# Narrower mask backgrounds, query masks by multiplication, and new engine orders in a fused delta-rule attention and MLP kernel

## The chip, the cores and the metric

The kernel runs on one core of a Trainium2 chip. The metric is the device time of one execution in microseconds (us); the program is one launch from inputs in device memory to the output in device memory.

## The reference

For each of 4 batches and 8 heads a state of 48x48 is carried over 768 time steps (a delta rule with a rate beta), and the result goes through an MLP with a tanh GELU:

```python
for t in range(S):                       # q, k, v: (4, 8, 768, 48); beta: (4, 8, 768)
    y[:, :, t] = einsum('bhd,bhde->bhe', q[:, :, t], state)
    v_old = einsum('bhde,bhd->bhe', state, k_n[:, :, t])      # k_n: k by its norm
    state = state + beta_t * einsum('bhd,bhe->bhde', k_n[:, :, t], v_t - v_old)
...
x = y.transpose(0, 2, 1, 3).reshape(3072, 384)
h = x @ w_in                             # (384, 2048)
out = gelu_tanh(h) @ w_out               # (2048, 384)
```

## The kernel before

The 768 steps are cut into 12 chunks of 64 steps. A chunk c has two units, u = 2c and 2c+1; a unit holds 8 head pairs (two batches share the 128 partitions, 64 steps each). For a unit, `prep(u)` scales k by its norm (`kn`), rounds q (`qb`), turns both (on TensorE as `Th`, L585 and L599, for the first six units, by DMA as `turn` after that), and multiplies k against k and q (`G`, L619) into two PSUM banks. From the banks VectorE takes three masked triangles into SBUF: `ln` (lower, k against k), the first half of `wp` (upper, k against k) and the second half of `wp` (upper, k against q; called `wq` in the list of dependences). A triangular system is then inverted in five rounds, each a product `A` (L693), an addition from PSUM on VectorE (`rt`, `rt16`, `rt32`, L700), a product `B` (L693) and a copy of the result (`bde` or `xi`, L421, on ScalarE or VectorE). For units 0 and 1 the same five rounds run in halves (`Ath`, `rth`, `Bth`, `xih`, L661, L666). `chain(c)` carries the state: products `K`, `Um`, `Q`, `S`, `O` (L739, L775, L784, L797) and their copies; for chunk 0 it is `R0`, `Uh`, `Oh`, then a turn `Xh` (L828) with the copy `xTh` (L832). `mlp(c)` multiplies the chunk's 256 rows with W1 (`up`, L852, 16 groups of three products of 256 columns for each chunk, four groups to a GELU on ScalarE, L857) and with W2 (`down`, L864, eight groups of four products of 384 columns), and `Z` and `out` copy and store it.

The triangles are taken with `copy_predicated`, which leaves what the mask does not choose as it was. So each of the six `wp` buffers (128 partitions x 8 heads x 128) and each of the four `ln` buffers (x 64) needs a background before its first use: the unit matrix in columns 0 to 63 and zeros in the columns of `wq`. These are the operations `triw` and `tri`, copies of a template `tmpl`, 128 columns wide, whose right half is zeroed on GpSimd by `tmplz`. They may stand on ScalarE, VectorE or GpSimd. GpSimd copies two bf16 as one float. `bdz` and `bez` zero the block matrices `bd` and `be` in the same stage.

Nothing is scheduled at run time. The table `ORDER` lists for each engine every operation in its order (`pe`, `act`, `dve`, `pool`, and `sp` for the DMA queue that loads and stores); `BANKS` gives the PSUM bank of each allocation in the order of the `pe` list. Every engine works strictly through its list and waits on semaphores for what an operation needs. In a name such as `up.3.5/2`, the number is a position in the program and what stands behind the slash counts operations of one name. `fill` is a product of zeros (L476) that TensorE does between the real ones; there are 61. GpSimd's list also starts the eight loads of W1 and W2 (`w1`, `w2`, L526 and L530; `w1.-3` is the first quarter of W1, read by `up.3`). Loads into the three buffers of q, k and v are in SP's list (`loadq`, `loadk`, `loadv`; `loadqr` for the first three chunks of q), and a load waits until its buffer has been read. A second program for negative beta lies behind a flag and does not run.

Of the kernel before, what the change touches and what calls it, by code (L numbers as in the profile page):

```python
# [5 lines left out]
F32 = mybir.dt.float32  # L6
BF16 = mybir.dt.bfloat16
U16 = mybir.dt.uint16
ALU = mybir.AluOpType
# [3 lines left out]
C = 64  # L13
# [5 lines left out]
        fill/8 fill/48 fill/21 fill/20 fill/47 fill/10 fill/52 fill/13 fill/30 fill/9 fill/55 betaT.-28/0 fill/58 fill/1 fill/46  # L19
        fill/43 fill/5 fill/16 fill/27 fill/18 fill/42 fill/12 Th.0/0 fill/0 Th.1/0 fill/23 fill/4 fill/33 Gh.0/0 Gh.1/0 fill/29  # L20
        fill/45 Th.3.01/0 Ath.0/0 Ath.1/1 fill/32 fill/25 Bth.0/0 fill/7 Th.2/0 fill/39 Bth.1/1 Ath.0/2 Ath.0/1 fill/51 Ath.1/0
        Ath.1/3 G.2/0 Bth.0/1 Bth.1/0 Th.3/0 Bth.0/2 Ath.1/2 Bth.1/3 fill/36 Ath.0/3 fill/59 fill/26 Ath.0/4 Ath.1/5 G.3/0 Bth.1/2
        A.2/0 Bth.0/3 Ath.1/4 fill/31 fill/54 fill/19 Bth.1/5 Ath.0/5 Bth.0/4 Bth.1/4 Th.1.01/0 Ath.1/7 fill/60 Bth.0/5 A.3/0
        Ath.0/6 Ath.0/7 B.2/0 fill/2 Bth.1/7 fill/44 Bth.0/7 Gh.1/1 Bth.0/6 Ath.1/6 B.3/0 A.2/1 Ath.0/9 Ath.0/8 fill/37 fill/22
        fill/28 B.2/1 Th.4/0 A.3/1 Ath.1/9 Bth.0/9 Bth.1/6 Bth.0/8 fill/57 A.2/2 B.3/1 Gh.0/1 Ath.1/8 Th.5/0 bminT.40/0 Th.5.01/0
        Bth.1/8 Bth.1/9 fill/15 fill/17 A.3/2 B.2/2 Uh.0.5/0 Uh.0.5/1 G.4/0 fill/53 Oh.0.7/0 Oh.0.7/1 fill/24 B.3/2 fill/41
        Xh.0.8/0 Xh.0.8/1 A16.2/0 fill/38 G.5/0 S.0.5/0 up.3.5/0 up.3.5/1 fill/11 A16.3/0 B.2/3 A.4/0 up.3.5/2 up.3.5/3 up.3/0
        up.3/1 up.3/2 up.3/3 B.3/3 up.3.25/0 up.3.75/0 up.3.25/1 up.3.25/2 A32.2/0 up.3.25/3 B.4/0 A.5/0 A32.3/0 B.2/4 up.3.75/1
        K.2.5/0 down.4.5/0 B.3/4 up.3.75/2 down.4.54/0 up.3.75/3 A.4/1 B.5/0 fill/3 down.4/0 Um.2.5/0 A.5/1 down.4.04/0 Q.2.6/0
        O.2.7/0 S.2.5/0 down.4.58/0 down.4.62/0 fill/50 B.5/1 down.4.08/0 B.4/1 A.5/2 down.4.12/0 A.4/2 K.4.5/0 B.5/2 up.5.75/0  # L30
        B.4/2 up.5.25/0 up.5.75/1 up.5.75/2 up.5.75/3 up.5.25/1 A16.5/0 up.5.25/2 A16.4/0 up.5.25/3 G.6/0 B.5/3 up.5.5/0 up.5.5/1
        up.5.5/2 B.4/3 G.7/0 up.5.5/3 up.5/0 up.5/1 up.5/2 A32.5/0 up.5/3 A32.4/0 A.6/0 fill/34 B.5/4 A.7/0 G.9/0 G.8/0 B.4/4
        B.6/0 down.6/0 down.6.04/0 B.7/0 down.6.08/0 Um.4.5/0 A.6/1 down.6.12/0 Q.4.6/0 S.4.5/0 O.4.7/0 B.6/1 A.8/0 A.7/1
        down.6.5/0 down.6.54/0 B.8/0 A.9/0 A.6/2 down.6.58/0 B.7/1 down.6.62/0 B.9/0 A.8/1 B.6/2 A.7/2 K.6.5/0 up.7.25/0 up.7.25/1
        up.7.25/2 B.8/1 A16.6/0 B.7/2 A.9/1 up.7.25/3 up.7/0 up.7/1 B.6/3 up.7/2 A16.7/0 up.7/3 A.8/2 up.7.75/0 B.9/1 up.7.75/1
        B.7/3 up.7.75/2 A32.6/0 B.8/2 G.10/0 up.7.5/0 up.7.75/3 up.7.5/1 A32.7/0 up.7.5/2 up.7.5/3 A16.8/0 G.11/0 B.7/4 B.6/4
        B.8/3 A.9/2 down.8.5/0 down.8/0 down.8.54/0 Um.6.5/0 A.10/0 B.9/2 down.8.04/0 Q.6.6/0 S.6.5/0 O.6.7/0 A16.9/0 A.11/0
        down.8.08/0 B.10/0 A32.8/0 B.9/3 down.8.12/0 K.8.5/0 B.11/0 down.8.58/0 A32.9/0 down.8.62/0 A.10/1 B.8/4 A.11/1 B.9/4
        up.9.75/0 up.9.75/1 up.9.75/2 B.10/1 up.9.75/3 Um.8.5/0 G.13/0 up.9.25/0 up.9.25/1 up.9.25/2 up.9.25/3 Q.8.6/0 A.10/2
        B.11/1 O.8.7/0 G.12/0 S.8.5/0 up.9.5/0 up.9.5/1 up.9.5/2 up.9.5/3 up.9/0 up.9/1 up.9/2 A.11/2 up.9/3 A.13/0 K.10.5/0  # L40
        B.10/2 B.11/2 A.12/0 down.10/0 up.11/0 up.11/1 up.11/2 up.11/3 B.12/0 B.13/0 A16.10/0 up.11.25/0 down.10.04/0 B.10/3
        up.11.25/1 A16.11/0 up.11.25/2 up.11.25/3 A.12/1 A.13/1 up.11.75/0 down.10.08/0 B.11/3 up.11.75/1 A32.10/0 B.12/1 B.13/1
# [12 lines left out]
        Um.16.5/0 up.17.5/1 up.17.5/2 up.17.5/3 Q.16.6/0 G.21/0 O.16.7/0 S.16.5/0 up.17.75/0 up.17.75/1 up.17.75/2 up.17.75/3
        A.18/2 up.17/0 up.17/1 up.17/2 up.17/3 up.17.25/0 up.17.25/1 A.20/0 A.19/2 up.17.25/2 up.17.25/3 B.18/2 up.19.25/0 A.21/0
        B.20/0 B.19/2 up.19.25/1 up.19.25/2 up.19.25/3 B.21/0 up.19/0 up.19/1 A16.19/0 down.18/0 A16.18/0 A.21/1 up.19/2 up.19/3
        A.20/1 B.19/3 down.18.04/0 B.18/3 B.20/1 down.18.08/0 G.22/0 K.18.5/0 B.21/1 down.18.12/0 up.19.5/0 down.18.5/0 up.19.5/1
        A.20/2 up.19.5/2 A.21/2 up.19.5/3 A32.18/0 A32.19/0 down.18.54/0 B.20/2 B.21/2 B.19/4 down.18.58/0 B.18/4 down.20.5/0
        A16.21/0 A16.20/0 down.18.62/0 Um.18.5/0 down.20.54/0 Q.18.6/0 G.23/0 S.18.5/0 O.18.7/0 down.20.58/0 down.20/0 A.22/0  # L60
        up.19.75/0 up.19.75/1 up.19.75/2 B.20/3 up.19.75/3 A.23/0 B.22/0 down.20.04/0 B.21/3 B.23/0 K.20.5/0 A32.20/0 down.20.08/0
        A.23/1 up.21.5/0 up.21.5/1 up.21.5/2 A32.21/0 up.21.5/3 B.20/4 A.22/1 B.23/1 B.21/4 down.20.62/0 down.20.12/0 up.21.25/0
        up.21.25/1 B.22/1 A.23/2 Um.20.5/0 up.21.25/2 up.21.25/3 Q.20.6/0 B.23/2 A.22/2 S.20.5/0 O.20.7/0 up.21/0 up.21/1 up.21/2
        up.21/3 B.22/2 up.21.75/0 A16.23/0 up.21.75/1 up.21.75/2 A16.22/0 up.21.75/3 K.22.5/0 down.22/0 down.22.04/0 B.23/3 B.22/3
        down.22.08/0 up.23/0 up.23/1 up.23.25/0 up.23/2 up.23/3 down.22.12/0 A32.23/0 up.23.25/1 A32.22/0 up.23.25/2 up.23.25/3
        down.22.5/0 B.23/4 up.23.5/0 down.24.5/0 B.22/4 up.23.5/1 down.22.54/0 down.22.58/0 down.24.54/0 up.23.5/2 up.23.75/0
# [279 lines left out]
def bass_deltanet__then__act_gelu_tanh_kernel(  # L346
# [9 lines left out]
    B, H, S, D = q.shape  # L356
# [658 lines left out]
```

## Time and profile before

| | |
|---|---|
| median of 3 runs | 249.84 us (250.45, 249.84, 246.84) |
| the profiled execution | 248.81 us, of which the span from first to last instruction is 247.1 us |
| busy, TensorE (PE) | 235.5 us, 95% of the span |
| busy, VectorE (DVE) | 193.5 us, 78% |
| busy, ScalarE (ACT) | 173.0 us, 70% |
| busy, GpSimd (POOL) | 147.9 us, 60% |
| granted TensorE clock | 1.00 throughout |

A busy share is a mean over stages: in the first 40 us the kernel loads, builds the masks and inverts the first units; from then on the products of the MLP stand between those of later units. The busy time of PE includes the products of zeros.

### The profile page before, as it was taken

What the parts mean: (1) busy time and instruction counts of PE and PEld (TensorE: products, weight loads), DVE (VectorE), ACT (ScalarE), POOL (GpSimd) and SP (SyncE); (2) the same over time, 40 slices, a digit from 0 to 9 for tenths busy, and PEclk for the clock granted to TensorE, in tenths of its full rate; (3) what the DMA queues carried; (4) which work ended last, traced back from release to release, by engine and by line L of the source; (5) the groups of instructions that cost most, each with busy time, mean ns of one, the idle gap of its engine ahead of it and who ended that gap; (6) DMA issues with size and microseconds to landing.
All of it is one profiled execution on the core that took longest, in us unless ns stands there. A gap on an engine that the chain in (4) does not pass through costs nothing.

```text
span 247.1 us, 11724 instructions
## 1 busy us (share of the span) xinstructions
PE 235.5 (95%) x5222; PEld 184.3 (75%) x5239; DVE 193.5 (78%) x340; ACT 173.0 (70%) x285; POOL 147.9 (60%) x224
## 2 busy tenths in 40 slices
PE   7778887999999999999999999999999999999995
PEld 3356776868878977888777888777887788877772
DVE  5999997888999999887898897999788897710200
ACT  6788887847988986877766795855684547655260
POOL 4099976659587888687879695985947332020000
PEclk9999999999999999999999999999999999999999
DMA  5999999999999998999979599728584012400142
GB/s 106 179 175 168 159 167 175 173 140 119 162 168 133 156 177 146 167 122 167 144 123 145 114 141 150 105 48 113 96 178 69 20 35 47 104 3 3 27 104 72
DMA packets 105063, 29.62 MB, mean 120 GB/s; under 512 B 96784, under 2 KB 104976, under 8 KB 105008
## 3 DMA queue, kind: packets, MB, share of 16 engines
q1 hardware_dynamic: 100640, 25.37, 65.9%
q0 software_dynamic: 3712, 3.15, 9.4%
q8 instruction: 43, 0.70, 1.3%
q10 hardware_dynamic: 656, 0.30, 0.5%
q14 instruction: 12, 0.10, 0.2%
HBM read 20.55 MB, written 4.72 MB: 102 GB/s over the span
## 4 chain that ended last, share of the span: by engine, by line
PE 87%; DVE 6%; ACT 2%; issue 2%; POOL 1%; POOLq 0%
PE ps L852 26%; PE ps L864 26%; PE ps L693 20%; PE ps L739 3%; PE ps L619 3%; PE ps L476 2%; PE ps L775 2%; PE ps L797 2%; PE ps L661 2%; PE ps L784 1%; DVE rt L700 1%; DVE nrm L546 1%; DVE rl L666 1%; POOL xi L650 1%; DVE wp L627 1%
## 5 line engine op out<-in xcount | busy, mean ns | idle before, releaser
L852 PE MATMUL ps<-xT,W 128*128 128x256 bf16 x576 | 77.5, 272 | 0.0
L864 PE MATMUL ps<-W,gT 128*128 128x384 bf16 x384 | 74.7, 326 | 0.4 <-issue 0.4
L421 ACT ACTIVATE bd<-ps 64x512 bf16<-64x512 f32 (+2 forms) x115 | 62.9, 561 | 12.6 <-PE ps L693 10.7
L857 ACT ACTIVATE gT<-ps 128x1024 bf16<-128x1024 f32 x48 | 48.7, 1021 | 19.7 <-PE ps L852 19.3
L852 PEld LDWEIGHTS ps<-xT,W 128*128 128x128 bf16 x576 | 50.7, 97 | 6.8
L700 DVE TENSOR_TENSOR rt<-ps,two 128x512 bf16<-128x512 f32 x66 | 44.1, 684 | 6.1 <-PE ps L693 5.4
L864 PEld LDWEIGHTS ps<-W,gT 128*128 128x128 bf16 x384 | 33.1, 97 | 16.8 <-issue 0.6
L687 POOL COPY be<-xi 64x256 f32<-64x256 f32 (+1 forms) x64 | 24.1, 382 | 31.5 <-ACT xi L421 19.0
L421 DVE CAST bd<-ps 64x512 bf16<-64x512 f32 (+2 forms) x41 | 26.3, 649 | 5.2 <-PE ps L693 4.7
L700 DVE TENSOR_TENSOR rl<-ps,two 128x384 bf16<-128x384 f32 (+1 forms) x44 | 20.8, 486 | 9.4 <-PE ps L693 8.8
L549 POOL TENSOR_TENSOR nrm<-nrm,half 128x16 f32<-128x16 f32 x9 | 26.4, 2936 | 2.8 <-DVE nrm L546 2.6
L683 POOL TENSOR_SCALAR_AFFINE_SELECT be<-ln 64x512 bf16<-64x512 bf16 x32 | 21.9, 684 | 10.2 <-DVE ln L640 5.5
L643 DVE CAST_PREDICATED wp<-mup,ps 128x1024 bf16<-128x1024 uint16 x22 | 26.7, 1212 | 0.5 <-PE ps L619 0.3
L421 ACT ACTIVATE xi<-ps 128x256 bf16<-128x256 f32 (+2 forms) x40 | 19.1, 492 | 10.8 <-PE ps L693 8.6
L576 POOL TENSOR_TENSOR tok<-kraw,nrm 128x384 bf16<-128x384 f32 x22 | 18.2, 832 | 6.6 <-PE ps L784 5.2
L693 PE MATMUL ps<-wp,be 128*128 128x64 bf16 (+1 forms) x384 | 18.2, 187 | 0.4 <-issue 0.3
L640 DVE CAST_PREDICATED ln<-mlo,ps 128x512 bf16<-128x512 uint16 x22 | 15.0, 687 | 4.5 <-PE ps L619 4.3
L693 PEld LDWEIGHTS ps<-wp,be 128*128 128x128 bf16 x384 | 15.5, 97 | 2.5 <-issue 0.6
L476 PE MATMUL ps<-wz 128*128 128x512 bf16 x44 | 14.4, 433 | 2.4 <-DVE braw L482 1.3
L421 ACT ACTIVATE ob<-ps 128x384 f32<-128x384 f32 x16 | 7.8, 489 | 12.4 <-PE ps L864 12.2
L693 PE MATMUL ps<-ln,bd 128*128 128x64 bf16 (+1 forms) x352 | 15.9, 188 | 0.1
L693 PEld LDWEIGHTS ps<-ln,bd 128*128 128x128 bf16 x352 | 13.8, 97 | 1.6
(119 smaller groups left out, 368.2 us busy)
## 6 DMA issues: line engine op xcount, KB each, us to landing
vraw<-in_v_dram SPq DMA_DIRECT2D x24, 192.0 KB, 4.8
out_dram<-ob SPq DMA_DIRECT2D x47, 96.0 KB, 3.1
kraw<-in_k_dram SPq DMA_DIRECT2D x22, 192.0 KB, 4.9
qraw<-in_q_dram SPq DMA_DIRECT2D x18, 192.0 KB, 5.1
W<-in_moe_w_out_dram POOLq DMA_DIRECT2D x4, 384.0 KB, 6.9
W<-in_moe_w_in_dram POOLq DMA_DIRECT2D x4, 384.0 KB, 6.5
qraw<-in_q_dram SPq DMA_DIRECT2D x12, 96.0 KB, 3.6
kraw<-in_k_dram SPq DMA_DIRECT2D x3, 96.0 KB, 3.6
```

What stands on the lines that cost most here:

```text
L421: return e.activation(out, in_, ACT.Copy) if e is nc.scalar else e.tensor_copy(out, in_)
L476: return e.matmul(P(f"fill{i}")[:, :], wz[:, 0:128], wz[:, 0:512])
L549: e.tensor_tensor(nr[:, 1, hx], nr[:, 0, hx], half[:, hx], ALU.pow),
L576: A("dve" if u < 2 else POOL, z + "kn", lambda e, P: e.tensor_tensor(kn, kr, nr[:, 3, hx].rearrange("t (p g) -> t p g", p=2).unsqueeze(3). ...
L643: A("dve", z + "wp", lambda e, P: e.copy_predicated(wp[s][:, :, :], mup[:, :].bitcast(U16).unsqueeze(1).to_broadcast([128, H, 2 * C]), P(p ...
L683: A("pool", z + "X1", lambda e, P, src=src, dst=dst: e.affine_select(out=dst, in_=src, compare_op=ALU.not_equal, fill=-1.0, base=0, patter ...
L687: A("pool", z + "bdc", lambda e, P, src=src, dst=dst: e.tensor_copy(dst.bitcast(F32), src.bitcast(F32)), reads=[w("xi")], writes=[xs[a]], ...
L693: ins = e.matmul(P(name)[:, C * h + to.start:C * h + to.stop], D_[:, h, :], rhs[:, h, to])
L700: A("dve", z + f"rt{lo or str()}", lambda e, P, i=i, to=LIVE[i], r_=r_: e.tensor_tensor(r_[:, :, to], P(ps(f"A{i}")).rearrange("p (h t) -> ...
L852: ins = e.matmul(P(ph)[:, w * f:w * f + w].rearrange("p (x t) -> p x t", x=2), W1[:, j, 128 * (i + f):128 * (i + f) + 128], x_[:, :, j, :] ...
L857: A("act", z + "gelu", lambda e, P, i=i, ph=ph: e.activation(g_[:, i:i + nf, 0:w], P(ph).rearrange("p (f t) -> p f t", f=nf), ACT.Gelu_app ...
L864: ins = e.matmul(P(po)[:, 0:DM], g_[:, f, 128 * b:128 * b + 128], W2[:, f, :], start=(f == 0), stop=(f == FC - 1))
```

## The change

The template is 64 columns wide and has no zero half, so `tmplz` is gone and `triw` writes columns 0 to 63 of a `wp` buffer only, 512 elements in a partition in place of 1024. In the first use of each buffer (units 0 to 5) the second half of `wp` is no longer taken with `copy_predicated`: it is multiplied with the mask, which writes zeros where the mask is zero and needs no background. For units 0 and 1 this replaces one operation by one (`wph`). For units 2 to 5 the one operation `wp` over 1024 elements becomes two over 512, `wp` and `wq`. From unit 6 on nothing is different: a buffer has its zeros from the first use.

```diff
-        tmpl = sb("tmpl", [128, 2 * C])
+        tmpl = sb("tmpl", [128, C])
...
-                A("pool", "0tmplz", lambda e, P: e.memset(tmpl[:, C:2 * C], 0.0), writes=["tmplz"], pos=-11)
...
-            for t, n, w in ((ln, "ln", C), (wp, "wp", 2 * C)):
+            for t, n, w in ((ln, "ln", C), (wp, "wp", C)):
...
-                        e, t[s][:, :, :], tmpl[:, 0:w].unsqueeze(1).to_broadcast([128, H, w])) if e is not nc.gpsimd else
-                      e.tensor_copy(t[s][:, :, :].bitcast(F32), tmpl[:, 0:w].bitcast(F32).unsqueeze(1).to_broadcast([128, H, w // 2])),
-                      reads=["tmpl", "tmplz"], writes=[f"{n}{s}"] + ([f"wq{s}"] if w > C else []), pos=2 * s - 9)
+                        e, t[s][:, :, 0:w], tmpl[:, 0:w].unsqueeze(1).to_broadcast([128, H, w])) if e is not nc.gpsimd else
+                      e.tensor_copy(t[s][:, :, 0:w].bitcast(F32), tmpl[:, 0:w].bitcast(F32).unsqueeze(1).to_broadcast([128, H, w // 2])),
+                      reads=["tmpl"], writes=[f"{n}{s}"], pos=2 * s - 9)
...
-                A("dve", z + "wph", masked(wp[s][:, :, C:2 * C], mup[:, 0:C], ps("Gq")), reads=["mup"], frees=[ps("Gq")], writes=[n("wq")], pos=u)
+                A("dve", z + "wph", lambda e, P: e.tensor_tensor(wp[s][:, :, C:2 * C].rearrange("p (x g) t -> p x g t", x=2), head(P(ps("Gq"))),
+                                                                 mup[:, 0:C].unsqueeze(1).unsqueeze(1).to_broadcast([128, 2, 4, C]), ALU.mult),
+                  reads=["mup"], frees=[ps("Gq")], writes=[n("wq")], pos=u)
...
+                if u < NP:
+                    gcols = lambda P, y: P(ps("G")).rearrange("p (h t) -> p h t", h=H)[:, :, C * y:C * y + C]
+                    A("dve", z + "wp", lambda e, P: e.copy_predicated(
+                        wp[s][:, :, 0:C], mup[:, 0:C].bitcast(U16).unsqueeze(1).to_broadcast([128, H, C]), gcols(P, 0)), reads=["mup"], frees=[ps("G")], writes=[n("wp")], pos=u)
+                    A("dve", z + "wq", lambda e, P: e.tensor_tensor(
+                        wp[s][:, :, C:2 * C], gcols(P, 1), mup[:, 0:C].unsqueeze(1).to_broadcast([128, H, C]), ALU.mult), reads=["mup"], frees=[ps("G")], writes=[n("wq")], pos=u)
+                else:
...
```

All five lists of `ORDER` and the table `BANKS` are replaced. Of the lists two lines stand for the rest:

```diff
-        masks.-12/1 masks.-12/0 half.-28/0 masks.-12/2 tmplz.-11/0 ident.-29/0 mup.-12/0 mup.-12/1 two.-12/0 ident2.-29/0
...
+        masks.-12/0 masks.-12/1 masks.-12/2 two.-12/0 two.-12/1 ident.-29/0 ident2.-29/0 mlo.-12/0 triw.-9/0 mlo.-12/1 triw.-7/0
...
```

There are 61 products of zeros in both. Between ScalarE, VectorE and GpSimd 116 operations change sides, most of them copies out of PSUM. Of the ten backgrounds `tri` and `triw`, GpSimd had one before and has seven now (five `triw`, two `tri`); ScalarE has the other three, and VectorE, which had four, has none.

Three places show what moves. The first is VectorE's list from the first use of the mask of unit 2 (`ln2`, `wp2`) to that of unit 3; `rt`, `xi` and `nrm` are other work, and the numbers behind names are those of buffers. Before:

```order
L640 COPY_PREDICATED ln2<-mlo0,ps 128x512
L643 COPY_PREDICATED wp2<-mup0,ps 128x1024
L421 CAST xi0<-ps 128x256
L666 TENSOR_TENSOR rt1<-ps,two0 128x256
L666 TENSOR_TENSOR rt0<-ps,two0 128x256 x2
L640 COPY_PREDICATED ln3<-mlo0,ps 128x512
L551 TENSOR_SCALAR nrm2<-nrm2 128x16
L700 TENSOR_TENSOR rt2<-ps,two0 128x512
L666 TENSOR_TENSOR rt1<-ps,two0 128x256 x2
L553 RECIPROCAL nrm2<-nrm2 128x16
L666 TENSOR_TENSOR rt0<-ps,two0 128x256
L643 COPY_PREDICATED wp3<-mup0,ps 128x1024
```

and now:

```order
L642 COPY_PREDICATED ln2<-mlo0,ps 128x512
L649 TENSOR_TENSOR wp2<-ps,mup0 128x8x64
L647 COPY_PREDICATED wp2<-mup0,ps 128x8x64
L675 TENSOR_TENSOR rt1<-ps,two0 128x256 x2
L675 TENSOR_TENSOR rt0<-ps,two0 128x256
L642 COPY_PREDICATED ln3<-mlo0,ps 128x512
L675 TENSOR_TENSOR rt0<-ps,two0 128x256
L647 COPY_PREDICATED wp3<-mup0,ps 128x8x64
...
L709 TENSOR_TENSOR rt2<-ps,two0 128x512
L649 TENSOR_TENSOR wp3<-ps,mup0 128x8x64
```

One operation of twice the width became two; for unit 3 the query half now comes later than the other.

The second is the head of GpSimd's list, up to the first `X1h` (L650 before, L659 now; it makes `xi` of unit 0). Before:

```order
L439 AFFINE_SELECT mup<-mup 64x128 x2
L446 AFFINE_SELECT two<-two 64x64
L429 AFFINE_SELECT ident<-ident 128x128
L446 AFFINE_SELECT two<-two 64x64
L443 AFFINE_SELECT mlo<-mlo 64x64 x2
L650 TENSOR_TENSOR xi<-ln,two 128x256
L555 TENSOR_TENSOR nrm<-nrm,bsb 128x16
```

and now:

```order
L462 COPY wp<-tmpl 128x8x32
L444 AFFINE_SELECT mlo<-mlo 64x64
L462 COPY wp<-tmpl 128x8x32
L436 MEMSET half 128x16
L470 MEMSET bd 128x1024
L440 AFFINE_SELECT mup<-mup 64x128
L530 DMA W<-in_moe_w_out_dram 128x4x384
L462 COPY ln<-tmpl 128x256
L555 TENSOR_TENSOR nrm<-nrm,bneg 128x8
L440 AFFINE_SELECT mup<-mup 64x128
L462 COPY wp<-tmpl 128x8x32 x2
L659 TENSOR_TENSOR xi<-ln,two 128x256 x3
```

Backgrounds (L462), the zeroing of a `bd` (L470), a step of unit 1's norms (L555) and the first load of W2 (L530) now stand ahead of it.

The third is TensorE's list around the first products with W1 (L852 before, L861 now), which wait for the copies `xTh` of the turned chunk 0 (L828, L837). Before:

```order
L828 MATMUL ps<-ident,xo 128x128 x6
L693 MATMUL ps<-ln,bd 128x48 x8
L476 MATMUL ps<-wz 128x512
L619 MATMUL ps<-kT 64x128 x16
L784 MATMUL ps<-us,tok 64x48 x32
L852 MATMUL ps<-xT,W 128x256 x6
```

and now:

```order
L837 MATMUL ps<-ident,xo 128x128 x6
L476 MATMUL ps<-wz 128x512
L861 MATMUL ps<-xT,W 128x256 x6
L619 MATMUL ps<-kT 64x128 x16
L702 MATMUL ps<-rl_2,bd 128x64 x8
L702 MATMUL ps<-ln,bd 128x48 x8
L861 MATMUL ps<-xT,W 128x256 x18
```

The first products of the MLP now stand ahead of `G` of unit 5 (L619) and of the state's product `S` (L784, further down now).

267 lines of the change are left out of this document (134 added, 133 removed), and 16 rows, old and new, of the table BANKS.

## The prediction

> **What bounds the kernel now.** I read the page's busy shares first, then its slices, then the busy time by stage, because the change touches the first 40 us only in its arithmetic but every stage in its orders.
>
> ```profile
> span 247.1 us, 11724 instructions
> PE 235.5 (95%) x5222; PEld 184.3 (75%) x5239; DVE 193.5 (78%) x340; ACT 173.0 (70%) x285; POOL 147.9 (60%) x224
> ...
> PE   7778887999999999999999999999999999999995
> ...
> DVE  5999997888999999887898897999788897710200
> ```
>
> TensorE is full from the seventh slice on, VectorE is full in slices 2 to 6. The stages, cut where this turns (first columns: length, then busy time and count of PE, PE weight loads, DVE, ACT, POOL):
>
> ```profile
> 10.00:34.00 24.00, 20.47 (x558) 15.36 (x568) 23.86 (x62) 20.31 (x48) 20.80 (x25) 1.00 1.15 167
> 34.00:40.00 6.00, 4.35 (x142) 3.24 (x141) 4.38 (x9) 4.89 (x10) 3.37 (x6) 1.00 1.29 184
> 40.00:50.00 10.00, 9.95 (x210) 8.56 (x209) 9.15 (x16) 8.35 (x12) 6.92 (x8) 1.00 1.41 167
> 50.00:75.00 25.00, 24.32 (x616) 19.02 (x616) 22.83 (x33) 19.11 (x30) 18.19 (x26) 1.00 1.01 146
> 75.00:100.00 25.00, 24.80 (x611) 20.55 (x609) 23.65 (x39) 21.04 (x36) 21.18 (x27) 1.00 1.03 157
> 100.00:125.00 25.00, 24.68 (x551) 20.61 (x549) 20.85 (x33) 19.75 (x30) 18.70 (x31) 1.00 1.02 149
> 125.00:243.00 118.00, 117.88 (x2527) 93.43 (x2526) 81.82 (x129) 72.66 (x110) 56.12 (x89) 1.00 0.47 83
> ```
>
> From 10 to 34 us VectorE works 23.86 of 24.00 us: this stage is as long as VectorE's list up to there. From 40 to 243 us TensorE idles 0.05 + 0.68 + 0.20 + 0.32 + 0.12 = 1.37 of 203 us: this stage is as long as TensorE's real work, which the change leaves alone. So only three things can move the end: when TensorE becomes full, the 1.37 us, and products of zeros that stand between real ones. In the 40 us before, PE's busy time is no work measure, since 44 recorded products of zeros are in it:
>
> ```profile
> L476 PE MATMUL ps<-wz 128*128 128x512 bf16 x44 | 14.4, 433 | 2.4 <-DVE braw L482 1.3 <-issue 0.5 <-DVE bsb L492 0.4
> ```
>
> **The change part by part.** First VectorE's stretch. It runs from the copy of the first turned k (`kTh` of unit 0) to the copy of the turned chunk 0 (`xTh`), behind which the MLP's first products stand in both orders:
>
> ```profile
> 10.96 0.42 DVE L421 COPY kT<-ps 128x512 bf16<-128x512 bf16 x1
> 37.82 0.56 DVE L421 COPY xT<-ps 128x384 bf16<-128x384 bf16 x2
> ```
>
> that is 26.86 us. What is in it, by rows:
>
> ```profile
> L643 DVE CAST_PREDICATED wp<-mup,ps 128x1024 bf16<-128x1024 uint16 x22 | 26.7, 1212 | 0.5 <-PE ps L619 0.3
> L627 DVE CAST_PREDICATED wp<-mup,ps 128x512 bf16<-128x512 uint16 x2 | 1.4, 686 | 0.0
> L700 DVE TENSOR_TENSOR rt<-ps,two 128x512 bf16<-128x512 f32 x66 | 44.1, 684 | 6.1 <-PE ps L693 5.4
> L752 DVE TENSOR_TENSOR rs<-ps,vraw 128x768 bf16<-128x768 f32 x11 | 10.5, 951 | 0.4 <-PE ps L739 0.4
> L421 DVE COPY wp<-tmpl 128x1024 bf16<-128x1024 bf16 x3 | 1.2, 422 | 0.6 <-ACT tmpl L456 0.6
> L421 DVE CAST bd<-ps 64x512 bf16<-64x512 f32 x21 | 14.4, 684 | 1.7 <-PE ps L693 1.4
> L421 DVE CAST xi<-ps 128x256 bf16<-128x256 f32 x4 | 1.7, 414 | 0.0
> L421 DVE COPY kT<-ps 128x512 bf16<-128x512 bf16 x3 | 1.2, 414 | 0.0
> L472 DVE MEMSET be<- 128x512 uint32 x2 | 1.0, 485 | 0.1
> ```
>
> The multiplication `wq` is not in this trace. Its bounds are a copy without PSUM, 0.42 us for twice the width, and the 768-wide operation from PSUM, 0.95 us; I take 0.684 us, the addition `rt`, which has the same width, the same source in PSUM and a second operand repeated over the heads. The narrower `wp` is 0.686 us. So a first use of units 2 to 5 costs 0.684 + 0.686 - 1.212 = +0.16 us, 0.63 us for all four (by the bounds -0.42 to +1.70), and for units 0 and 1 nothing (0.684 for 0.686). Three of the four lie in the stretch: +0.48. The new list puts three more `bde` there (+2.05) and one `binv` (0.17), and takes out one `xih` (0.41), one `kTh` (0.41), one wide background (0.42), one `bez` (0.48) and one reciprocal (0.24). The sum is +0.74 us of durations. All durations of the stretch add up to 31.0 us in 26.86 us of time, as neighbours overlap, so 0.74 counts 0.64; I take **+0.6**, with -0.5 and +1.5 as ends from the bounds of `wq`.
>
> Before the stretch VectorE was not full: what set the time was ScalarE, whose backgrounds stood ahead of the first squares. From the chain of waits:
>
> ```profile
> 4.05 0.63 ACT ln L421
> 4.68 0.95 ACT wp L421
> 5.63 0.42 ACT sq L544
> 6.07 0.55 DVE nrm L546
> ```
>
> The two backgrounds leave ScalarE's place here and go to GpSimd, whose list had nothing to do until 12.65 us. That frees 1.58 us, but the squares need k:
>
> ```profile
> 0.79 0.74 ACTq L518 DMA_DIRECT2D kraw<-in_k_dram  x1
> 1.57 0.63 ACTq L483 DMA_DIRECT2D braw<-in_beta_dram  x1
> ...
> kraw<-in_k_dram ACTq DMA_DIRECT2D x1, 96.0 KB, 3.1
> ```
>
> ScalarE now issues beta ahead of its piece of k, so this starts near 1.57 and lands near 4.7, and SP has a piece of q ahead of the others. The first square can start about 0.7 us earlier than at 5.53, the second (its pieces are SP's third and fourth, one issue later) not. VectorE does three more zeroings (`bdz`, 0.48 each) here, in time in which it waited. I take **-0.5** for `kTh`; the ends are -1.4, where only VectorE's own list counts, and +0.8, one issue on SP, where the second k pieces decide.
>
> Then the turn into the full stage:
>
> ```profile
> 38.33 0.41 PE L619 MATMUL ps<-kT 48*64 48x128 bf16 x13
> 39.85 0.25 PE L619 MATMUL ps<-kT 48*64 48x128 bf16 x3 [1.11 <-issue]
> ```
>
> TensorE stops 1.11 us inside `G` of unit 5, between two products that wait for nothing; no engine releases it. What it is, the trace does not say; I suppose that instructions came late. It can come again at another place or not at all, so I count half: **-0.55** (0 to -1.1). In the new order the first products with W1 stand ahead of this `G`, which only exchanges work within a full engine. Behind the first `up` there were five products of zeros before the last ones of the program, now there are four; three of them cost 0.65 us in the chain:
>
> ```profile
> 11.04 0.65 PE ps L476 x3
> ```
>
> so **-0.2**. Work that moves between engines after 40 us I cost at nothing: it is covered by TensorE's full queue, and without the cover each us of idling there is a us of time.
>
> Sum: +0.6 - 0.5 - 0.55 - 0.2 = -0.65 us. The profiled execution took 248.81 us with 247.1 us of span; the sum on it gives 248.2. It lies 1.0 below the median shown, 249.84, and the mean of it and the three runs is 249.0, which I take as base: **248.3 us**.
>
> **The rivals.** *(a) The early W2 load holds up k.* GpSimd now starts a quarter of W2 behind the sixth piece of its list; from the release of the template at 4.05 us and what stands between I estimate 6.5 us, where it was 20.7 at the earliest. How loads fare without and with weights in flight show the issues from 5 to 15 us and from 18 to 36 us (size, us to landing):
>
> ```profile
> kraw<-in_k_dram SPq DMA_DIRECT2D x6, 192.0 KB, 4.2
> ...
> W<-in_moe_w_in_dram POOLq DMA_DIRECT2D x4, 384.0 KB, 6.5
> kraw<-in_k_dram SPq DMA_DIRECT2D x3, 192.0 KB, 8.0
> ...
> ACT sq L544 <- DMA kraw<-in_k_dram: 0.9, 1, 0.9
> ```
>
> The square of chunk 1 waited 0.9 us for k already, and now stands ahead of `kTh` of unit 1 on ScalarE and of all of VectorE's masks. If k of chunk 1, issued about 4 to 5.3 us, takes 8.0 instead of 4.2 us, it lands at 13.3, 3.3 us behind 10, from where on it decides: 248.3 + 3.3 = 251.6. For it speaks the doubled landing, against it that this k has a lead of more than 1 us. In the Trainium skill, "DMA: Bandwidth & Descriptors", section "Queues, rings and completion order", each DMA engine takes turns between the queues that have work, a packet at a time; by that rule any load beside the weights loses about half its rate, whoever was first. The landing times agree (8.0 for 4.2); by it alone the rival would be the forecast, were the weights issued together with k.
>
> *(b) The cover breaks in the full stage.* From 40 to 125 us VectorE works 76.5 of 85 us. New orders and new banks can put TensorE behind copies that come late; a twentieth of these 85 us is +4.3: 252.6 or more. Against it: the totals by engine hardly move (VectorE gains 0.63 and loses three backgrounds of 0.42).
>
> *(c) Everything comes.* Head -1.4, gap -1.1, zeros -0.2, stretch 0, idling of the full stage -1.2: 249.0 - 3.9 = 245.1. Against it: VectorE's stretch got longer by count.
>
> *(d) Nothing comes.* The second half of k decides, and the gap stays: 0.6 - 0.2 = +0.4: 249.4.
>
> **How the numbers follow.** The forecast has 0.45 (its own range 246.8 to 249.9), (a) 0.17, (b) 0.10, (c) 0.13, (d) 0.15. The low end, 245.0, is (c); the high end, 253.4, holds (a) and half of (b). A measurement of this kernel can tell about 2% from no change, 5 us. Faster by that needs all of (c) and a little more: 0.07. Slower needs the worse half of (b), or (a) with a second delay: 0.13. Within: 0.80.
>
> **What would show it.** Right: first `up` between 37.5 and 39.5 us (40.34 before), `kTh` of unit 0 near 10.4, `wq` 0.68 and narrow `wp` 0.69 us, VectorE over 95% busy from 11 to 34 us, TensorE idle under 1.6 us from 40 to 243. Wrong: a wait of ScalarE or VectorE on a k load before 16 us (a), PE idle of several us after 40 (b), or VectorE with gaps before 34 us, which would mean that another engine, GpSimd with its longer list, sets the first stage.

## The result, and the profile after

The change makes the kernel slower by a little over one per cent: 253.0 us median of 20 runs (249.67 to 258.62) against 248.21 us (246.84 to 250.45, 20 runs); the ratio is 1.0115, with a 95% interval from 1.0084 to 1.0146. The forecast was 248.3 us, slightly faster than the 249.0 that it took as base. Ten of the change's 20 runs, the profiled one of 254.62 us among them, stand more than 1.5% above its fastest and are left out of the ratio, which is therefore smaller than that of the medians (1.019).

The page's head and slices for the changed kernel:

```profile
span 252.9 us, 11719 instructions
PE 236.5 (94%) x5225; PEld 184.9 (73%) x5239; DVE 194.7 (77%) x341; ACT 170.0 (67%) x283; POOL 148.7 (59%) x228
...
PE   7788866989999997999999999999999999999995
...
PEclk9999988999999999999999999999999999999999
```

The work is the same (PE 236.5 us busy for 235.5), the span is 5.8 us longer, TensorE has holes in slices 6, 7 and 16, and its granted clock is below full in slices 6 and 7, which it is nowhere in the profile before. By stage (length, then busy time and count of PE, PE weight loads, DVE, ACT, POOL; granted clock, DMA share, GB/s):

```profile
10.00:34.00 24.00, 20.96 (x551) 14.82 (x558) 23.52 (x58) 18.99 (x47) 19.15 (x27) 1.00 1.08 177
34.00:40.00 6.00, 3.76 (x98) 3.05 (x99) 3.55 (x8) 3.47 (x6) 2.22 (x2) 0.72 1.45 171
40.00:50.00 10.00, 7.85 (x164) 6.24 (x165) 6.56 (x13) 6.97 (x11) 5.29 (x9) 1.00 1.29 173
50.00:75.00 25.00, 24.09 (x545) 19.00 (x544) 21.84 (x35) 18.48 (x30) 18.95 (x21) 1.00 0.78 125
75.00:100.00 25.00, 23.36 (x646) 19.55 (x644) 21.83 (x34) 20.96 (x35) 20.86 (x30) 1.00 0.96 147
100.00:125.00 25.00, 24.80 (x577) 20.35 (x573) 20.79 (x33) 19.46 (x32) 19.90 (x31) 1.00 0.81 140
125.00:243.00 118.00, 117.88 (x2591) 95.06 (x2591) 88.30 (x140) 73.39 (x113) 56.57 (x93) 1.00 0.49 85
```

Up to 34 us all is as forecast: VectorE is full (23.52 of 24.00). Then every engine has holes at once, between 34 and 50 us, so no engine is waiting for a busier one. From 40 to 243 us TensorE idles 2.15 + 0.91 + 1.64 + 0.20 + 0.12 = 5.02 us, where it was 1.37. Where it stops, by the timeline of TensorE (start, length, what, count, and in brackets the idle time ahead):

```profile
36.29 0.22 PE L670 MATMUL ps<-rl,xi 64*64 64x64 bf16 x2 [1.58 <-issue]
...
41.92 0.81 PE L861 MATMUL ps<-xT,W 128*128 128x256 bf16 x6 [0.28 <-ACT xT L422]
...
44.70 0.36 PE L619 MATMUL ps<-kT 48*64 48x128 bf16 x12 [1.79 <-issue]
...
51.55 0.71 PE L861 MATMUL ps<-xT,W 128*128 128x256 bf16 x5 [0.86 <-issue]
...
99.14 0.38 PE L806 MATMUL ps<-us,wp 64*64 64x48 bf16 x25 [1.50 <-issue]
```

The second of these lines is the first `up`; the other four are stops. Each of them is in the midst of a group of equal matmuls, and no engine releases it: it is the stop of 1.11 us at 39.85 us in the profile before, four times, 5.73 us in sum. The account nearly closes: the first `up` starts at 41.92 instead of 40.34 us (+1.58; that this is also the size of the first stop is chance, since the clock told of below enters too), and from 40 us on TensorE idles 3.65 us more, of which some 0.3 us lie ahead of that `up`: together about 5 of the 5.8 us.

What the stops have in common shows when the time is cut where TensorE resumes. The counts of PE and PE weight loads between two resumptions, for the changed kernel:

```profile
36.28:44.69 8.41, 5.60 (x125) 4.26 (x126) 4.37 (x9) 4.63 (x9) 3.22 (x5) 0.80 1.39 170
44.69:51.54 6.85, 5.99 (x126) 5.12 (x127) 5.91 (x11) 6.00 (x8) 3.61 (x6) 1.00 1.31 171
51.54:99.13 47.59, 45.89 (x1136) 37.25 (x1138) 42.59 (x65) 37.52 (x61) 37.40 (x47) 1.00 0.86 137
```

That is 251, 253 and 2274 = 9 x 252.7 instructions. TensorE stops after about 253 recorded instructions or a multiple of it (a few records and the waits are missing in the count). The profile also has a DMA queue for instructions, here for the whole program and for the 1.6 us from 33.2 us on, in which the first of the stops begins:

```profile
q8 instruction: 42, 0.69, 1.2%
```

```profile
q1 hardware_dynamic: 756, 0.14, 84.1%
q0 software_dynamic: 99, 0.10, 58.6%
q8 instruction: 1, 0.02, 5.8%
```

42 packets of 16 KB carry TensorE's 5225 + 5239 instructions, 66 bytes each: one packet is one block of about 250 instructions, and the packets come all through the run. (The Trainium skill, "Trainium Architecture — The Big Picture", section "The software stack", has instructions of 64 bytes; the 66 here agree, as a few records are missing in the count.) In the second window one packet is served beside loads that keep the DMA engines at 84% + 59%; 5.8% of 16 engines and 1.6 us is 1.48 us for this packet. By the trace's list of packets it starts at 33.26 us, TensorE reaches the end of its block at 34.7 and resumes at 36.29; for the other three stops the packet starts at 41.39, 48.67 and 96.49 us. TensorE resumes 2.7 to 3.3 us behind the start, as in the profile before (packet 36.87, resumed 39.85); over the stops of 0.4 us or more in all profiles it is 2.2 to 3.6 us.

On top comes the clock. TensorE in the 8 us around the first stop, changed kernel:

```profile
34.00:36.00 2.00, 0.71 (x15) 1.00 1.38 163
36.00:38.00 2.00, 1.35 (x31) 0.62 1.35 200
38.00:40.00 2.00, 1.69 (x56) 0.53 1.63 150
40.00:42.00 2.00, 1.64 (x33) 1.00 1.42 192
```

The means 0.62 and 0.53 make 1.52 + 1.88 = 3.4 us at half clock, at once behind the stop, from 36.48 to 39.89 us; up to 1.7 us of work at full clock are lost there. The Trainium skill, "TensorE: Matmul & The Clock Gate", section "What's actually happening", tells of a window of 3413 ns that runs freely, after an idle one of which TensorE gets half clock. The length agrees. That a whole window must be idle does not: the stop here is 1.58 us, and TensorE was at work on both sides of it. Nor is it the length of the stop alone, since the longer one of 1.79 us is not followed by half clock. Cut into stretches of 3.41 us, counted from 36.48 us, where the half clock begins, the profile shows why (length, then busy time of PE first):

```profile
33.07:36.48 3.41, 1.83 (x53) 1.04 (x51) 1.84 (x4) 2.22 (x4) 3.15 (x2) 1.00 1.39 175
43.31:46.72 3.41, 2.02 (x40) 1.80 (x41) 1.60 (x3) 1.26 (x3) 0.59 (x2) 1.00 1.18 150
```

The stretch ahead of the half clock holds 1.58 us of idle time; the stop of 1.79 us is cut by the border at 43.31, and the stretch behind that border holds 1.39 us. Cut in the same way, the profiles below show half clock behind every stretch with 1.6 us or more of idle time and full clock behind every one with 1.5 us or less; with 1.58 us they show both. (The run with SP's list alone, told of below, is left out: there half clock once followed 1.14 us.)

### The profile page after: what moved, and what is told of

It reads as the page before. It is cut to its first block, busy times and chain, and to the rows that moved or that the text cites. A ratio compares the mean times of both kernels' runs of the same rounds, so it can differ in the third digit from the quotient of the medians.

```text
span 252.9 us, 11719 instructions
## 1 busy us (share of the span) xinstructions
PE 236.5 (94%) x5225; PEld 184.9 (73%) x5239; DVE 194.7 (77%) x341; ACT 170.0 (67%) x283; POOL 148.7 (59%) x228
## 4 chain that ended last, share of the span: by engine, by line
PE 82%; DVE 11%; issue 4%; POOL 1%; ACT 0%; POOLq 0%
PE ps L873 25%; PE ps L861 24%; PE ps L702 19%; PE ps L748 3%; PE ps L619 3%; PE ps L784 2%; PE ps L806 1%; PE ps L476 1%; DVE rt L709 1%; DVE rt L675 1%; PE ps L793 1%; PE ps L670 1%; DVE bd L470 1%; POOL be L692 1%; DVE wp L649 1%
## 5 line engine op out<-in xcount | busy, mean ns | idle before, releaser
L861 PE MATMUL ps<-xT,W 128*128 128x256 bf16 x576 | 77.3, 272 | 1.1 <-issue 0.9
L873 PE MATMUL ps<-W,gT 128*128 128x384 bf16 x384 | 73.8, 326 | 0.0
L422 ACT ACTIVATE bd<-ps 64x512 bf16<-64x512 f32 (+2 forms) x111 | 60.6, 564 | 18.0 <-PE ps L702 16.6
L861 PEld LDWEIGHTS ps<-xT,W 128*128 128x128 bf16 x576 | 50.7, 98 | 8.4 <-issue 1.0
L696 POOL COPY be<-xi 64x224 f32<-64x224 f32 (+1 forms) x64 | 24.6, 391 | 28.6 <-ACT xi L422 22.3
L692 POOL TENSOR_SCALAR_AFFINE_SELECT be<-ln 64x512 bf16<-64x512 bf16 x32 | 21.0, 657 | 18.4 <-DVE ln L642 11.5
L422 DVE CAST bd<-ps 64x512 bf16<-64x512 f32 (+2 forms) x45 | 28.3, 639 | 3.5 <-PE ps L702 3.0
L652 DVE CAST_PREDICATED wp<-mup,ps 128x1024 bf16<-128x1024 uint16 x18 | 21.8, 1210 | 0.7 <-PE ps L619 0.7
L476 PE MATMUL ps<-wz 128*128 128x512 bf16 x47 | 15.9, 424 | 2.3 <-DVE wz L428 1.9
L702 PE MATMUL ps<-wp,be 128*128 128x64 bf16 (+1 forms) x384 | 17.1, 188 | 0.3 <-POOL be L696 0.2
L702 PE MATMUL ps<-ln,bd 128*128 128x48 bf16 (+1 forms) x352 | 15.9, 188 | 0.0
L758 POOL TENSOR_TENSOR vraw<-vraw,bsb 128x768 f32<-128x768 f32 x9 | 13.3, 1474 | 2.7 <-DMA vraw<-in_v_dram 2.4
```

Of the source, the lines that this page charges most:

```text
L422: return e.activation(out, in_, ACT.Copy) if e is nc.scalar else e.tensor_copy(out, in_)
L476: return e.matmul(P(f"fill{i}")[:, :], wz[:, 0:128], wz[:, 0:512])
L652: A("dve", z + "wp", lambda e, P: e.copy_predicated(wp[s][:, :, :], mup[:, :].bitcast(U16).unsqueeze(1).to_broadcast([128, H, 2 * C]), P(p ...
L692: A("pool", z + "X1", lambda e, P, src=src, dst=dst: e.affine_select(out=dst, in_=src, compare_op=ALU.not_equal, fill=-1.0, base=0, patter ...
L696: A("pool", z + "bdc", lambda e, P, src=src, dst=dst: e.tensor_copy(dst.bitcast(F32), src.bitcast(F32)), reads=[w("xi")], writes=[xs[a]], ...
L702: ins = e.matmul(P(name)[:, C * h + to.start:C * h + to.stop], D_[:, h, :], rhs[:, h, to])
```

## The experiments

Four theories. **A, late instructions:** the new order runs through its blocks of 250 instructions faster than the next ones come while loads keep the DMA engines full. **B, VectorE's stretch:** the four operations more on VectorE delay the first stage. **C, the early W2 load** (rival (a) of the prediction). **D, the stops belong to the work at which they stand.** Ratios below are to the kernel before, measured on the same chip.

**Arithmetic and orders apart.** First the new sums in the old orders and banks:

```diff
  lists and banks of the kernel before, code of the changed one; pool: -tmplz.-11/0
  dve:  wp.2/0 +wq.2/0   wp.3/0 +wq.3/0   wp.4/0 +wq.4/0   wp.5/0 +wq.5/0
```

> The orders and banks of before with the narrow backgrounds and the multiplied query masks alone (each wq stands right behind its wp, and the zeroing of the template's right half is left out). Theory, late instructions: the changed kernel lost its time in stops of TensorE at every 256th of its instructions, which come from the orders; this kernel should stop as before does, and take the time of before to within 1 us, 247.5 to 249.3. Rival, VectorE's stretch: the four wq at 0.68 us make the first stage longer than the prediction counted; then this kernel takes 250.5 or more, most of the loss of the change.

249.56 us, ratio 1.0016 (0.9976 to 1.0056): 0.3 us above what A expected, and 0.9 below what B did. Then the old sums in the new orders:

```diff
  lists and banks of the changed kernel, code of the one before; pool: +tmplz.-11/0
  dve:  -wq.2/0 -wq.3/0 -wq.4/0 -wq.5/0
```

> The orders and banks of the change with the old masks (wide backgrounds, no wq, the template zeroed on GpSimd). Theory, late instructions: stops of 1 to 2 us of TensorE at instructions 1209, 1463 and 1719 as in the changed kernel, and a time of 251 to 254. Rival, VectorE's stretch: 248 to 249, the time of before, since the multiplications are gone.

253.48 us, ratio 1.0148 (1.0079 to 1.0217). The arithmetic costs nothing that can be measured and the loss is that of the orders: B falls. The stops over 0.5 us in the second kernel's waits (engine, line, releaser; total, times, longest) and the stage in which its clock fell:

```profile
PE ps L811 <- issue: 1.7, 1, 1.7
PE ps L675 <- issue: 0.6, 1, 0.6
```

```profile
75.00:100.00 25.00, 23.26 (x543) 0.93 0.84 135
```

Two of the change's four stops are there: L675 is the group of its first, L811 that of its fourth. At the other two places TensorE runs on, though A expected them all. In the first kernel, which has TensorE's list of before, there are stops too, 1.54, 0.56 and 0.55 us, at the ends of other blocks than the one at 39.85 us, and none is followed by a lower clock. So the end of a block is a place where a stop can come, and it does not come there in every run.

**The early W2 load.**

```diff
  pool:  mup.-12/0 -w2.-1.7/0 tri.-9/0 ... w2.-1.9/0 +w2.-1.7/0 eps.6/0
```

> The changed kernel with the early load of a quarter of W2 moved from the seventh place behind the masks to the end of the eight weight loads. Rival, early weights: k of chunk 1 lands sooner, the copy of the first turned k starts nearer 9.5 us, and the time falls by 2 to 3 us. Theory, late instructions: the stops behind 34 us stay and the time is that of the changed kernel to within 1 us (its undisturbed runs were about 251.4).

252.54 us, ratio 1.0083 (1.0037 to 1.0129): the interval overlaps that of the change (1.0084 to 1.0146). Of C little or nothing is left; stops of 1.79 us at 41.81 us and 2.16 us at 97.28 us remain, at the places of the change's second and fourth.

**SP's list alone.**

```diff
  lists and banks of the changed kernel, but sp: the list before;
  act: -loadk.-40/0 +loadk.-40/1
```

> The changed kernel with the loads and stores of the DMA queue in the order of before. If instructions are late because the changed order of loads puts more traffic in their way between 28 and 52 us, the stops at instructions 1209, 1463 and 1719 shrink to what before has (one of 1.1 us) and the time falls by 2 to 4 us, to about 249. If they are late because TensorE's own list reaches the end of its blocks sooner, the stops stay and the time stays within 1 us of the changed kernel.

281.51 us, ratio 1.1288 (1.1218 to 1.1358), which nobody had expected and which says little on the question. The waits of TensorE and GpSimd:

```profile
PE ps L716 <- POOL be L710: 14.9, 3, 6.1
```

```profile
POOL tok L436 <- DMA qraw<-in_q_dram: 12.0, 3, 5.2
...
POOL sq L559 <- DMA kraw<-in_k_dram: 7.0, 1, 7.0
```

Loads stand in SP's list behind stores that the other lists now finish later; GpSimd waits for q and k, and TensorE for GpSimd. The lists only fit together as a set, so the order of the loads alone is not told apart. TensorE's list alone was not tried either, so whether it is TensorE's order or that of the loads that makes the stops stays open.

**Quiet DMA engines.** The loads of chunks 3 and later are cut to a sixteenth, in the changed kernel and in the one before; every instruction of every engine stays.

```diff
-                    js = slice(0, 2 * H) if x is None else slice(x, 2 * H, 2)
+                    js = (slice(0, 2 * H) if c < 3 else slice(0, 1)) if x is None else slice(x, 2 * H, 2)
```

> The changed kernel, whose loads of q, k and v for chunks 3 and later bring one head column of sixteen (so most of the input is left out of the computation; every instruction of the engines stays). Theory 'late instructions': TensorE's instructions come in blocks of 256 (128 matmuls) over the same DMA engines as the data, a block that TensorE runs through in about 4 us while loads are heavy ends before the next block is there, and in the changed kernel the blocks between 30 and 55 us are the shorter ones. With little loaded the blocks come at once: the stops without releaser of over 0.5 us (5.7 us in the profile of the change) fall to under 1.5 us in sum, no stretch at half clock, 247 to 249. Rival 'the order itself' (TensorE's list is so arranged that it waits, loads or not): the stops stay, 251 to 254.

> The kernel before with the same loads cut (chunks 3 and later bring one head column of sixteen; the rest of the input is left out). Theory 'late instructions': its stops of 1.1 and 0.35 us go, 246 to 247.5, so that the changed kernel with the same cut stands within 1.5 us of it, where without the cut 3 lay between them. Rival 'the order itself': 248, and the distance of some 3 us to the changed kernel stays.

247.55 us, ratio 0.9956 (0.9928 to 0.9984), and 248.08 us, ratio 0.9933 (0.9894 to 0.9971): the intervals overlap, so the two kernels no longer differ by more than the noise, though the second lies 0.6 us above what A expected of it. In the profile of the one before no stop without a releaser over 0.3 us is left; but three of its 12 runs have a mean clock of 0.993, so a stop that brings half clock still came in some. The stages of the changed one, and the largest stops in its waits:

```profile
34.00:40.00 6.00, 5.63 (x155) 4.09 (x150) 5.08 (x12) 5.24 (x12) 4.32 (x6) 1.00 1.12 159
40.00:50.00 10.00, 10.00 (x218) 8.32 (x216) 9.29 (x16) 9.56 (x14) 8.32 (x10) 1.00 0.51 77
```

```profile
PE ps L819 <- issue: 1.3, 1, 1.3
```

The three stops between 34 and 52 us are gone, TensorE is full from 40 to 75 us, and none of the 12 runs of the changed kernel had a stretch at half clock. This is the plainest answer: with all loads the new orders cost 1.15%, with few loads nothing that can be measured. The fourth stop stays (1.28 us, resumed at 92.11), however, and stays at the same matmuls of the same `O` group. The DMA engines from 86 to 91 us, in 40 slices:

```profile
DMA  3210299770000000000000000006000000000000
...
q1 hardware_dynamic: 160, 0.11, 11.6%
q8 instruction: 1, 0.02, 1.5%
```

They are idle from 87.3 us on; the single 6 is the packet of instructions, at 89.5 us, 3.4 us after TensorE had entered the block before (86.1). So full DMA engines are not the only thing that makes a block start late.

**Other ends of the blocks.** 32 small matmuls ahead of the first warm-up matmul (`fill/60` in the changed kernel, `fill/8` in the one before) move all ends by 64 instructions:

```diff
             def fill(e, P, i):
+                for x in range(32 if i == 60 else 0):
+                    e.matmul(P(f"fill{i}")[:, 0:8], wz[:, 0:128], wz[:, 0:8])
                 return e.matmul(P(f"fill{i}")[:, :], wz[:, 0:128], wz[:, 0:512])
```

> The changed kernel with 32 matmuls of 8 columns ahead of its first warm-up matmul, in time in which TensorE waits anyway; all blocks of 256 instructions then begin 64 instructions earlier in the work. From the starts in the profile of the change (stops taken out) the block that then begins at about 51 us takes 2.3 us to run, where 4.0 is the shortest there without the shift, and one near 110 us takes 1.9. Theory 'late instructions': the stops at 36, 45 and 52 us leave their places in the work and stand 64 instructions earlier, new ones of 1.5 to 3 us come at the ends of those two short blocks, 255 to 258. Rival 'the stops belong to the work at which they stand' (a wait that the profile does not show): they stay at the same matmuls, 252.5 to 253.5.

> The kernel before with the same 32 small matmuls ahead of its first warm-up matmul. Its blocks between 30 and 50 us keep 4 to 6 us each, but the one that then begins at about 51 us takes 3.3 us, and one near 108 us 1.5. Theory 'late instructions': the stop of 1.1 us at 39.85 us leaves its place, new ones of 1 to 3 us come at the ends of the two short blocks, 250 to 253. Rival 'the stops belong to the work': 248 to 249.

258.38 us, ratio 1.0409 (1.0356 to 1.0461), and 255.63 us, ratio 1.0250 (1.0194 to 1.0305). These 0.9 us of small matmuls cost 2.9% in the changed kernel (1.0409 by 1.0115) and 2.5% in the one before, twice what the whole change does. A part may be the head: `kTh` of unit 0 comes at 11.24 for 10.14 us in the changed kernel, and at 11.21 for 10.96 us in the one before. The largest stops of the kernel before, shifted:

```profile
33.75 0.55 PE L601 MATMUL ps<-ident,tok 128*128 128x128 bf16 x7 [0.64 <-issue]
...
38.70 0.26 PE L695 MATMUL ps<-rt,bd 128*128 128x64 bf16 x3 [0.81 <-issue]
...
56.67 0.21 PE L786 MATMUL ps<-us,tok 64*64 64x48 bf16 x3 [1.63 <-issue]
...
108.41 0.22 PE L786 MATMUL ps<-us,tok 64*64 64x48 bf16 x4 [0.73 <-issue]
...
179.97 0.21 PE L786 MATMUL ps<-us,tok 64*64 64x48 bf16 x3 [1.58 <-issue]
```

The old stop at `G` of unit 5 is gone, new ones came, the largest at the end of the block that begins at 51 us, as expected (3.3 us to run). The last one shows something that A does not have: the packet started at 177.53 us, 1.7 us after TensorE had entered the block before, no later than most, and from 177.8 us on the DMA engines are nearly idle; but that block took only 2.5 us to run. So a short block can end in a stop though its successor is not held up by loads. Another of 0.88 us stands at 132.31, and in the changed kernel three of 0.45 to 0.69 us stand behind 130 us. In the changed kernel the largest is 2.74 us, at 40.86 us, and the two blocks named as short end in stops of 1.05 us (58.35) and 0.69 us (111.40), smaller than the 1.5 to 3 expected. Its counts between resumptions are 254, 759 = 3 x 253 and 2023 = 8 x 252.9, though the stops stand at other matmuls: D falls. The shifted kernels cost more than the stops in their one profile add up to (the changed one: 5.4 us more by median, 3.0 by the spans of the profiles). The clock, at 0.987 or below in four of its six runs, has a part in it.

**Filling the stop.** Four warm-up matmuls ahead of the first stop, between 32.2 and 33.6 us, are done three times:

```diff
             def fill(e, P, i):
+                if i in (36, 11, 17, 3):
+                    for x in range(2):
+                        e.matmul(P(f"fill{i}")[:, :], wz[:, 0:128], wz[:, 0:512])
```

> The changed kernel; four of its warm-up matmuls between 32.2 and 33.6 us (0.22 us each) are done three times, so that TensorE has 1.76 us more to do in the block of instructions at whose end the profile of the change shows the stop of 1.58 us and, after it, 3.41 us at half clock. Theory 'late instructions, and half clock on top where the stop is long': the next block comes when it did, so the added matmuls only fill the stop; it shrinks to under 0.6 us, the matmuls after it start between 36.0 and 36.6 us as before, and the half clock at 36.5 to 39.9 us falls away, which is worth up to 1.7 us: 251 to 253, and more of the runs at a mean clock of 1.0 (3 of 20 for the change). Rival 'the stop belongs to the work': stop and added matmuls add up, 254.5 to 255.5.

253.89 us, ratio 1.0215 (1.0168 to 1.0262). Between the two expectations, and no gain:

```profile
36.78 0.19 PE L705 MATMUL ps<-wp,bd 128*128 128x64 bf16 x1 [1.33 <-issue]
...
97.43 0.18 PE L796 MATMUL ps<-us,tok 64*64 64x48 bf16 x1 [1.61 <-issue]
```

```profile
36.50:40.00 3.50, 2.92 (x108) 1.00 1.39 186
96.00:98.00 2.00, 0.57 (x40) 1.00 1.09 163
98.00:100.00 2.00, 2.00 (x36) 0.51 0.21 46
100.00:102.00 2.00, 2.00 (x60) 0.64 0.68 116
```

The 1.76 us of added matmuls went mostly into the stop: TensorE resumes 0.5 us later than in the change, and the clock stays full there. But the stop is still 1.33 us, not under 0.6, since the next packet came no earlier; and the half clock (0.98 + 0.72 = 1.7 us lost) came behind the stop at 97.43 us instead. All six runs had such a stretch. Filling this one stop with products of zeros did not buy back what it costs.

**A shift the other way.** The first eight warm-up matmuls become 120 small ones, so that the ends move by 224, which is 32 instructions the other way:

```diff
+                if i in (60, 10, 2, 25, 13, 9, 55, 26):
+                    for x in range(14):
+                        e.matmul(P(f"fill{i}")[:, 0:8], wz[:, 0:128], wz[:, 0:8])
+                    return e.matmul(P(f"fill{i}")[:, 0:8], wz[:, 0:128], wz[:, 0:8])
```

> The changed kernel; its first eight warm-up matmuls of 512 columns are replaced by 120 of 8 columns (together 3.4 us as before), so that the ends of all blocks move by 224 instructions, which is 32 the other way. From the starts in the profiles no block between 30 and 60 us then takes less than 4.0 us (3.9 in the change, 2.3 with the shift by 64). Theory 'what counts is which work falls into one block': 251 to 254, as the change itself. Rival 'more instructions, or more small matmuls at the start, cost by themselves' (64 of them went with 5.4 us): 224 cost more than that, 258 or above.

257.25 us, ratio 1.0367 (1.0309 to 1.0425): my expectation of 251 to 254 fails, and the rival's 258 is missed by less than 1 us, so that more instructions at the start cost something by themselves is not excluded. (The profiled execution, 254.75 us, was the shortest of the six; where the others lost 1 to 5 us more no trace shows.) The largest stops:

```profile
37.06 0.21 PE L778 MATMUL ps<-rs,xi 64*64 64x48 bf16 x2 [2.06 <-issue]
...
77.06 0.34 PE L810 MATMUL ps<-us,wp 64*64 64x48 bf16 x18 [1.42 <-issue]
99.19 0.25 PE L810 MATMUL ps<-us,wp 64*64 64x48 bf16 x9 [1.84 <-issue]
```

The first stands at the end of a block that took about 4.7 us to run, longer than many that pass without a stop; its packet started at 34.60 us, 4.3 us after TensorE had entered the block. So the length of a block does not decide alone. Over all profiles the start comes 0.2 to 5.1 us after the entry (mostly 1 to 2; 2.5 to 5.1 ahead of the stops between 30 and 50 us), and a stop is about this delay plus 3 us less the block's own length. What sets the delay is not settled: quiet DMA engines shorten it (at most 2.9 us up to 80 us in the kernel with small loads), but not everywhere.

**The clock by runs.** Each run's span was recorded with its mean clock, and a stretch of 3.4 us at half clock lowers the mean by 0.007. 45 runs of the kernel before were taken beside the first eight experiments, not beside those of the change (a forty-sixth took 785 us and is left out): 39 had no such stretch (0.996 or above), with a mean span of 247.0 us, and six had one (0.990 to 0.993), with 250.2 us. So half clock comes in the kernel before too, in one run of eight. Of the change's 20 runs four had none (249.6 us), eight one (0.991 to 0.993; 250.3 us), seven two (0.985 to 0.987; 253.7 us) and one three (256.9 us): 251.7 us in the mean, 4.7 above the 247.0. Some 2.6 us of it stand in runs without half clock (only four, from 247.9 to 253.4 us) and so go to stops at full clock; the rest comes with the half clock, at up to 1.7 us a stretch, and with the longer stops that bring it.

A version that beats both kernels was not found: with small loads, where nearly all stops are gone, the old orders are 0.7% faster than with all of the loads, and that is, as an estimate, about all that could be had from the stops.

## Why the prediction was wrong

- **The gap of 1.11 us** is the step that failed. It was the term "-0.55": a stop that may come again or not, counted half. The supposition behind it, that instructions came late, was right; but a thing that can happen at every block of the program was sized by the single time that it had happened, and its ends, 0 to -1.1, left no room for more stops than that one. The term measured +4.6 us in the profiled execution (5.73 of stops for 1.11); with the same list for TensorE it is +1.2 in the profile of the orders alone (0.57 + 1.72) and +2.8 in that with W2 late (1.79 + 2.16). The half clock, up to 1.7 us a stretch, comes on top and has no term in the sum.
- **"Work that moves between engines after 40 us I cost at nothing: it is covered by TensorE's full queue."** This failed with it. The cover held against engines: behind 40 us no group of TensorE's waits for VectorE, ScalarE or GpSimd exceeds 0.4 us. It did not hold for TensorE's own instructions, which no list shows.
- **VectorE's stretch, +0.6**: the operations cost what was estimated (`wq` 0.684 by the rows below, narrow `wp` 0.683, to 0 and 3 ns), and the experiment with the sums alone bears out that they are worth nothing measurable in the end. The stretch itself, from start to start, came out at 41.46 - 10.14 = 31.3 us where it was 26.9, since VectorE too stood still behind TensorE's stop from 34.7 us on; its list set the stage only up to there. With few loads, where that stop is missing, it is 27.4 us (10.15 to 37.56) for 26.9 us in the kernel before (11.71 to 38.62): +0.5, so the term was right.

```profile
L649 DVE TENSOR_TENSOR wp<-ps,mup 128x512 bf16<-128x512 f32 x4 | 2.7, 684 | 2.8 <-PE ps L619 2.8
L647 DVE CAST_PREDICATED wp<-mup,ps 128x512 bf16<-128x512 uint16 x4 | 2.7, 683 | 0.0
...
10.14 0.42 DVE L422 COPY kT<-ps 128x512 bf16<-128x512 bf16 x1
...
41.46 0.36 DVE L422 COPY xT<-ps 128x384 bf16<-128x384 bf16 x1 [0.55 <-PE ps L837]
```

- **The head, -0.5**: `kTh` of unit 0 came 0.82 us earlier (10.96 to 10.14), inside the ends given. It is hardly more than the spread: over the profiles without a shift it is 10.49 to 11.71 us with the old lists and 10.14 to 10.54 us with the new. What was gained was lost 24 us later.
- **Base and product of zeros**: the base was 0.8 us high (248.21 by 20 runs for 249.0); -0.2 is too small to be seen. (TensorE's row of slices is full from the eighth on, not the seventh; nothing hangs on it, as the stages were cut by time.)
- **The rivals**: (a) did not occur, moving the load back changes little. The sign named for it did show: before 16 us ScalarE waits 1.7 us for k, in two waits, where it was 0.9 us in one. But it is 1.7 us with the load moved back, too, and `kTh` of unit 0 came no later. (b) has the right place, TensorE idle after 34 us, and nearly the right time (252.6 and more, 253.0 measured) by a wrong mechanism: not copies that come late, but instructions. (c) and (d) let the stop vanish or stay as it was; neither came.
- **What would show it wrong** named "PE idle of several us after 40", and so it was. The range, 245.0 to 253.4, held the median by 0.4 us, and within 2% had 0.80; the direction was wrong. That the range held is luck: its upper end was made of rivals that did not come about as they were told.

## What to carry to other kernels

An unexplained stop of TensorE in the midst of a group of equal matmuls is not noise: count the instructions between two of them, and if the count is a constant, every block of that size is at risk. Here two things brought a stop: a block that is run through in a short time (2.5 us), loads or not, and a packet that starts late (2.5 to 5.1 us after the block before is entered), mostly with loads in flight. Compare orders by where these ends fall, too: the three shifts tried here, which leave the work as it is, cost 2.5 to 2.9%, and two sets of lists with the same work differ by 1.15%. An experiment that only thins the loads helps to tell such a cost from one of the order itself.

## What the runs showed of the hardware

- TensorE's instructions come over the data's DMA engines, 16 KB a packet and 66 bytes an instruction; where TensorE stops at the end of a block, it resumes 2.2 to 3.6 us after the next packet's start (stops of 0.4 to 2.7 us).
- A stop of 1.6 us, with TensorE at work before and behind it, can bring 3.4 us at half clock (0.62 and 0.53 in two windows of 2 us). It did so where 1.58 us or more of idle time fell into one stretch of 3.41 us (with one exception at 1.58), and two longer stops that were cut by a border of such stretches did not: 1.79 us in the change and 2.16 us with W2 late, with 1.39 and 1.27 us of idle time in the stretch that held most.
- 64 instructions more at the start made the kernel before 2.5% slower.
